# A planner's figures, a weight ring of six-block pieces and an ordered memory sum in a fused attention and MLP kernel

## Chip, cores, metric

One core of a Trainium2 chip. The metric is the device time of one execution in microseconds, median of several. Before: 692.45 us (3 runs, 692.03 to 692.54). The granted TensorE clock was 1.0.

## The reference, cut

A layer norm of `x` (2048 x 1024, bf16), then two branches whose results are added to `x`:

```python
xn = _layernorm(x)
# branch A: 32 heads of 32, four segments of 512 tokens with a running memory
q, k, v = xn @ wq, xn @ wk, xn @ wv
for s in range(4):
    p = softmax(qs @ ks.T * scale + causal mask); a_dot = p @ vs
    a_mem = (phi(qs) @ M) / (phi(qs) @ z + 1e-6)
    o = g * a_mem + (1 - g) * a_dot
    M += phi(ks).T @ vs ; z += sum(phi(ks))
# branch B: an MLP over the token axis, 2048 -> 3584 -> 2048
u = gelu(layernorm(xn).T @ w1 + b1); y = (u @ w2 + b2).T
return x + o @ wo + y
```

## The kernel before

A program on the host fixes the order of all instructions of all engines before anything runs. It keeps a clock for each engine (`fw.now`), books a duration for each instruction and each transfer, and at every point lets TensorE do what is ready by these books. I call this program the planner and its durations the books. From 214 us on, TensorE has two kinds of work: the attention chain (projections, bursts of logits, weighings), which waits for ScalarE, VectorE and POOL, and the fill: the matmuls of 32 output sums, whose w2 part by then needs only its weights, and whose wo part also an attention result. A gap in the chain is filled with fill matmuls.

Some words used below: a **row block** is 128 rows of w2, the weights of one fill matmul; a **piece** is what one transfer loads, four or six row blocks; a **ring** is the set of buffers that pieces pass through. A **burst** is the run of short matmuls that makes one step's logits, a **weighing** multiplies the exponentials with v, the **ost copy** evacuates its bank to SBUF, the **memory sum** adds that bank's `phi(k).T@v` to M and z. Cut to what the change touches:

```python
def dma(...):                                    # books of one transfer
    start = max(self.now[issuer], self.ready(reads, writes))
    self.now[issuer] = start + 450               # the issue
    self.q_free = max(start + 1900, self.q_free) + nbytes / 320 + (700 if transpose else 0)
    self.settle(self.q_free + 100 + ..., reads, writes)     # the landing
# ...
self.w2r = [e.take(f"w2n{i}", [P, 4, P], BF16) for i in range(6)]   # ring N of w2 pieces
self.w2l = [e.take(f"w2l{i}", [P, 6, P], BF16) for i in range(3)]   # ring L, sums worked on in single steps
# _Ring.ensure(b): when piece b is first asked for, load up to piece b + depth
# weigh(u, qb): a bank gets p@v, phi(q)@M and, in the last quarter of a segment, phi(k).T@v
fl.op({"dve": (tensor_copy ps->ost, 150 + n * 35, ...),   # whichever engine is free first by the books
       "act": (activation Copy ps->ost, 230 + n * 27, 200 + n * 27)}, [], [self.R_ost[o][qb]], box=box, give=not upd)
if upd:                                                   # memory sum, from the same bank
    fl.op({"dve": (MZ32 += ps, 283, 320)}, [self.R_MZ32[g]], [self.R_MZ32[g]], box=box, give=True)
```

`give=True` is where the books return the bank. A rule beneath all this makes readers of one bank on different engines wait for each other with semaphores; the planner's books did not contain that rule.

The softmax here doesn't subtract the row's maximum and nothing guards it: scores larger than these inputs give would overflow.

Of the kernel before, what the change touches and what calls it, by code (L numbers as in the profile page):

```python
# [18 lines left out]
P = 128  # L19
# [84 lines left out]
class FW:  # L104
# [121 lines left out]
    def dma(self, out_ap, in_ap, reads=(), writes=(), is_output=False, issuer="sp", extra=(),  # L226
            record_reads=True, transpose=False):
        es = self.E[issuer]
        nbytes = 2
        for x in out_ap.shape:  # L230
            nbytes *= x
        start = max(self.now[issuer], self.ready(reads, writes))
        self.now[issuer] = start + 450
        self.q_free = max(start + 1900, self.q_free) + nbytes / 320 + (700 if transpose else 0)
        self.settle(self.q_free + 100 + (600 if transpose else 0), reads, writes)
        self.log[issuer].append((start, self.q_free - start, writes[0].name if writes else ""))
        if not is_output:
            i = self.dma_next
            while self.dma_counts[i] and not self.slot_waiters[i]:
                i = (i + 1) % self.N_DMA_SEMS  # L240
            self.dma_next = (i + 1) % self.N_DMA_SEMS
            extra = list(extra) + self.slot_waiters[i]
            self.slot_waiters[i] = []
        self._waits(es, reads, writes, extra)
        assert not (es.pending_slots and issuer != "sp"), f"issuer {issuer} waited pool dma sem"
        es.pending_slots = []
        ins = es.eng.dma_start(out_ap, in_ap, transpose=True) if transpose else es.eng.dma_start(out_ap, in_ap)  # L247
        if is_output:
            j = self.out_next
            assert j < self.N_OUT_SEMS, "too many output dmas"  # L250
            self.out_next += 1
            ins.then_inc(self.out_sems[j], 16)
            tok = _Tok(("outdma", j), self.out_sems[j], 16)
            self.out_toks.append(tok)
        else:
            self.dma_counts[i] += 16
            ins.then_inc(self.dma_sems[i], 16)
            tok = _Tok(("dma", i), self.dma_sems[i], self.dma_counts[i])
        self._record(tok, reads if record_reads else (), writes)
        return tok  # L260
# [105 lines left out]
class _Flow:  # L366
# [1 line left out]

    LOOK = 5
    MARGIN = 120  # L370
    MARGIN_STEP = 80
    PART = 200

    def __init__(self, fw, R_bank, free, fill):
        self.fw, self.R_bank, self.free, self.fill = fw, R_bank, free, fill
# [208 lines left out]
class _Kernel:  # L584
# [95 lines left out]
    def over_early(self):  # L680
        fw = self.fw
        e = _Arena(self.nc, self.early_base, self.early_end)
        wait = _after(*self.R_xin, *self.R_xnt)
        self.wv_sb = e.take("wv_sb", [P, N_DCH, D_MODEL], BF16)
        self.wqr = [e.take(f"wq{i}", [P, N_DCH, P], BF16) for i in range(2)]
        self.wkr = [e.take(f"wk{i}", [P, N_DCH, P], BF16) for i in range(2)]
        self.w2r = [e.take(f"w2n{i}", [P, 4, P], BF16) for i in range(6)]
        self.w2l = [e.take(f"w2l{i}", [P, 6, P], BF16) for i in range(3)]
        self.w2s = [e.take(f"w2s{i}", [P, P], BF16) for i in range(2)]
        self.prod = e.take("prod", [P, 4, P], BF16)  # L690
        self.R_prod = Res("prod", wait)
        self.o_s = [e.take(f"o_s{i}", [P, 4, P], BF16) for i in range(2)]
        self.R_os = [Res(f"o_s{i}", wait) for i in range(2)]
        self.R_wv = [Res(f"wv{i}", wait) for i in range(2)]
        self.R_wq = [Res(f"wq{i}", wait) for i in range(2)]
        self.R_wk = [Res(f"wk{i}", wait) for i in range(2)]
        self.R_w2 = [Res(f"w2n{i}", wait) for i in range(6)]
        self.R_w2l = [Res(f"w2l{i}", wait) for i in range(3)]
        self.R_w2s = [Res(f"w2s{i}", wait) for i in range(2)]
        self.pkT = e.take("pkT", [P, SEG_L], BF16)  # L700
        self.etmp = e.take("etmp", [P, SEG_L], BF16)
        self.R_pkT = Res("pkT", wait)
        self.R_etmp = Res("etmp", wait)
        self.wq_ring = _Ring(fw, [t[:] for t in self.wqr], self.R_wq)
        self.wk_ring = _Ring(fw, [t[:] for t in self.wkr], self.R_wk)
        for i in range(N_UNIT):
            g = i % N_GRP
            self.wq_ring.srcs.append(self.A_wq[:, g * P:(g + 1) * P].rearrange("(dc p) j -> p dc j", p=P))
            self.wk_ring.srcs.append(self.A_wk[:, g * P:(g + 1) * P].rearrange("(dc p) j -> p dc j", p=P))
        self.fill = _Fill(self)  # L710
        self.wq_ring.ensure(0)
        self.wk_ring.ensure(0)
        for bv in range(2):
            fw.dma(self.wv_sb[:, :, bv * 512:(bv + 1) * 512],
                   self.A_wv[:, bv * 512:(bv + 1) * 512].rearrange("(dc p) j -> p dc j", p=P), writes=[self.R_wv[bv]])
# [311 lines left out]
        return self.flow.pe(mms, [R_w] + self.R_xnT[4 * s:4 * s + 4])[0]  # L1027

    def evac(self, dst, R_dst, box, view=lambda x: x):
        self.flow.op({"act": (lambda e, b: e.activation(dst, view(self.bank(b)), ACT.Copy), 635, 560),  # L1030
                      "dve": (lambda e, b: e.tensor_copy(dst, view(self.bank(b))), 690, 727)},
                     [], [R_dst], box=box, give=True, prio=0)

# [68 lines left out]
    def step(self, items):  # L1102
# [44 lines left out]
        pT, R = self.pT, self.R_pT  # L1147
        for i, (r, blocks, slot, masks) in enumerate(items):
            fl.op({"act": (lambda e, b, slot=slot: e.activation(pT[:, slot, :], self.bank(b), ACT.Exp, scale=SCALE),  # L1149
                           620, 530)}, [], [R[slot]], box=box[i], give=True)  # L1150
            v = pT[:, slot, :].rearrange("p (j q) -> p j q", q=P)
            if len(masks) > 1:
                ap, pat = v[:, masks[0]:masks[1] + 1:masks[1] - masks[0], :], [[0, 2], [1, P]]
            else:
                ap, pat = v[:, masks[0], :], [[1, P]]
            ns = 180 + 115 * len(masks)
            fl.op({"pool": (lambda e, ap=ap, pat=pat: e.affine_select(ap, ap, pattern=pat, compare_op=ALU.is_ge,  # L1157
                                                                      fill=0.0, base=0, channel_multiplier=-1),
                            ns, ns + 30)}, [R[slot]], [R[slot]])

    def weigh(self, u, qb):
# [19 lines left out]
        def mms(b):  # L1181
# [9 lines left out]
            if upd:  # L1191
# [5 lines left out]
        n = 8 if s else 4  # L1197
        dst = self.ost[o][:, 8 * qb:8 * qb + n, :].rearrange("p a x -> p (a x)")
        fl.op({"dve": (lambda e, b: e.tensor_copy(dst, self.ps[:, b, 0:n * VW]), 150 + n * 35, 185 + n * 35),  # L1199
               "act": (lambda e, b: e.activation(dst, self.ps[:, b, 0:n * VW], ACT.Copy), 230 + n * 27, 200 + n * 27)},  # L1200
              [], [self.R_ost[o][qb]], box=box, give=not upd, prio=0)
        if upd:
            m32, mbf = self.MZ32[:, g, :], self.MZbf[:, g, :]
            dg = self.diag[:].rearrange("p r x -> p (r x)")
            if s == 0:
                fl.op({"dve": (lambda e, b: e.tensor_copy(m32, self.ps[:, b, 2 * GW:3 * GW]), 283, 320)},
                      [], [self.R_MZ32[g]], box=box, give=True, prio=0)
            else:
                fl.op({"dve": (lambda e, b: e.tensor_tensor(m32, m32, self.ps[:, b, 2 * GW:3 * GW], op=ALU.add), 283, 320)},
                      [self.R_MZ32[g]], [self.R_MZ32[g]], box=box, give=True, prio=0)  # L1210
            fl.op({"dve": (lambda e: e.tensor_tensor(mbf, m32, dg, op=ALU.mult), 296, 330)},
                  [self.R_MZ32[g], self.R_diag], [self.R_MZbf[g]], prio=2)

    def combine(self, u):
# [17 lines left out]
        else:  # L1232
# [7 lines left out]
            for k, to, R_to in ((0, os, R_os), (1, self.prod, self.R_prod)):  # L1240
# [1 line left out]
                rk = rec.rearrange("p (q k r) -> p q k r", q=4, k=2)[:, :, k, :].unsqueeze(3)  # L1242
                pk = to[:].rearrange("p q (r d) -> p q r d", d=D_HEAD)
                dve(lambda e, v=v, rk=rk, pk=pk: e.tensor_tensor(pk, v, rk.to_broadcast([P, 4, 4, D_HEAD]), op=ALU.mult),
                    R_ost + [R_rec], [R_to], 640)
            dve(lambda e: e.tensor_tensor(os[:], os[:], self.prod[:], op=ALU.add), [R_os, self.R_prod], [R_os], 424)
        oT, R_oT = self.oT[s % 2], self.R_oT[s % 2][g]
        R_old = self.R_xnT[0:4] if s == 1 else []
# [9 lines left out]
    def attention_and_out(self):  # L1258
# [43 lines left out]
                else:  # L1302
                    break
        goals = [0, 0]
        knots = [(0, 0)] + [(last[8 * s + 7] + 2, 222 + 285 * s) for s in range(3)]
        knots += [(len(steps) - 1, self.fill.total - self.RESERVE), (len(steps), self.fill.total - 3)]
        for i in range(1, len(steps) + 1):
            (x0, y0), (x1, y1) = next((k0, k1) for k0, k1 in zip(knots, knots[1:]) if k0[0] <= i <= k1[0])
# [163 lines left out]
class _Fill:  # L1472
    KEEP = 5
    PLAIN = 12
    SOON = 600

    def __init__(self, k):
        self.k = k
        self.closed = []
        long = []  # L1480
        rest = [(c, half, False, 0) for c in range(12, 16) for half in range(2)]
        for j in range(3):
            g = [(c, half, True) for c in range(4 * j, 4 * j + 4) for half in range(2)]
            long += [x + (1,) for x in g[:3]]
            rest += [x + (0,) for x in g[3:]]
        long[-1] = long[-1][:3] + (0,)
        self.L = _Stream(k, self, long, "L", k.w2l, k.R_w2l, 2, [3])
        self.N = _Stream(k, self, rest, "N", k.w2r, k.R_w2, 4, [0, 1, 2])
        self.streams = [self.L, self.N]
        self.total = self.L.total() + self.N.total()  # L1490

# [107 lines left out]
```

## Time and profile before

| | before |
|---|---|
| time, us | 692.45 |
| span of the profile, us | 690.6 |
| PE / ACT / DVE / POOL busy, us | 685.7 / 299.7 / 241.2 / 152.8 |
| holes between 20 us and the tail, us | 1.23 (from the matmuls' starts) |

How to read it: a **hole** is what two neighbouring TensorE instructions start further apart than the same pair does undisturbed. The busy share hides holes under 163 ns; the prediction shows why, and shows the lines.

### The profile page before, as it was taken

The numbers are of one execution on the slowest core, as the hardware profiler recorded it, in microseconds if no ns is written. First come the engines' busy times: TensorE is split into PE (matmuls) and PEld (weight loads), VectorE is DVE, ScalarE is ACT, GpSimd is POOL, SyncE is SP. The second block draws the span as 40 slices with busy tenths as digits, with TensorE's granted clock in tenths as the row PEclk, the third lists the DMA queues.
The fourth block names the chain that finished last, engine by engine and source line by source line (L and its number), as shares of the span: only waits on it lengthen the run. The fifth ranks groups of instructions, "written<-read, shape, count | busy, mean of one in ns | idle before, by whom it ended". The sixth has DMA issues, their size and how long they took to land.

```text
span 690.6 us, 12093 instructions
## 1 busy us (share of the span) xinstructions
PE 685.7 (99%) x4846; PEld 328.2 (48%) x4846; DVE 241.2 (35%) x545; ACT 299.7 (43%) x571; POOL 152.8 (22%) x379
## 2 busy tenths in 40 slices
PE   8999999999999999999999999999999999999998
PEld 3444444444444544544455444544545544454544
DVE  6731100000002433443454462643534633351535
ACT  7331111111136456565365335644744644544540
POOL 5820000000001233223133113312321322313230
PEclk9999999999999999999999999999999999999999
DMA  9367666325037557656556556455554445637334
GB/s 316 112 178 183 158 159 204 94 61 138 1 100 168 137 126 175 142 136 157 119 131 150 118 129 150 97 138 136 140 130 116 119 104 136 148 86 130 92 78 141
DMA packets 275698, 92.04 MB, mean 133 GB/s; under 512 B 234171, under 2 KB 272059, under 8 KB 275643
## 3 DMA queue, kind: packets, MB, share of 16 engines
q1 hardware_dynamic: 275642, 91.28, 53.5%
q8 instruction: 38, 0.62, 0.4%
q14 instruction: 18, 0.14, 0.1%
HBM read 74.47 MB, written 5.24 MB: 115 GB/s over the span
## 4 chain that ended last, share of the span: by engine, by line
PE 97%; ACT 1%; DMA 1%; POOL 0%; DVE 0%; issue 0%; SPq 0%; POOLq 0%; DVEq 0%
PE ps_all L217 97%; DMA w2n<-in_B_w_dram 1%; ACT xn_tmp L849 0%; DMA xin<-in_A_x_dram 0%; ACT xn_tmp L851 0%; POOL pT L1157 0%; DVE h L890 0%; ACT pT L1149 0%; POOL ln_r L882 0%; SPq L247 0%; POOLq L580 0%; DVE fin L1342 0%; POOL ln_t L880 0%; DVE ln_mv L865 0%; DVEq L65 0%
## 5 line engine op out<-in xcount | busy, mean ns | idle before, releaser
L1157 POOL TENSOR_SCALAR_AFFINE_SELECT pT<-pT 128x256 bf16<-128x256 bf16 (+1 forms) x320 | 126.4, 403 | 507.7 <-ACT pT L1149 497.5
L1149 ACT ACTIVATE pT<-ps_all 128x512 bf16<-128x512 f32 x320 | 163.7, 614 | 76.8 <-PE ps_all L217 76.8
L217 PE MATMUL ps_all<-h,w1all 128*128 128x512 bf16 x896 | 193.9, 379 | 0.8 <-DVE h L890 0.7
L217 PE MATMUL ps_all<-gT,w2n 128*128 128x512 bf16 x644 | 151.3, 379 | 0.2 <-DMA w2n<-in_B_w_dram 0.2
L217 PEld LDWEIGHTS ps_all<-h,w1all 128*128 128x128 bf16 x896 | 87.5, 98 | 107.2 <-DMA w1all<-in_B_w_dram 1.0
L1004 ACT ACTIVATE gT<-ps_all,bc 128x512 bf16<-128x512 f32 x56 | 37.7, 690 | 140.7 <-PE ps_all L217 140.7
L217 PEld LDWEIGHTS ps_all<-gT,w2n 128*128 128x128 bf16 x644 | 59.6, 98 | 68.4 <-issue 3.1
L217 PE MATMUL ps_all<-gT,w2l 128*128 128x512 bf16 x244 | 63.7, 380 | 0.0
L217 PE MATMUL ps_all<-xnT,wq 128*128 128x512 bf16 x256 | 60.5, 379 | 0.0
L217 PE MATMUL ps_all<-xnT,wk 128*128 128x512 bf16 x256 | 60.5, 379 | 0.0
L217 PE MATMUL ps_all<-wv_sb,xnT 128*128 128x512 bf16 x256 | 60.1, 379 | 0.0
L1462 DVE SCALAR_TENSOR_TENSOR stg<-ps_all,bc,stg 128x512 bf16<-128x512 f32 x32 | 24.0, 750 | 99.2 <-PE ps_all L217 99.1
L217 PEld LDWEIGHTS ps_all<-vA,pT 128*128 128x128 bf16 x1280 | 45.3, 96 | 15.5 <-POOL pT L1157 0.6
L217 PE MATMUL ps_all<-vA,pT 128*128 128x33 bf16 x1280 | 46.3, 177 | 0.1
L1200 ACT ACTIVATE ost<-ps_all 128x264 bf16<-128x264 f32 (+1 forms) x56 | 19.8, 366 | 58.2 <-PE ps_all L217 57.1
L942 DVE TENSOR_SCALAR gcol<-gcol 128x32 f32<-128x32 f32 x1 | 0.2, 181 | 118.5 <-ACT gcol L940 118.5
L217 PEld LDWEIGHTS ps_all<-wv_sb,xnT 128*128 128x128 bf16 x256 | 25.0, 98 | 30.2
L217 PEld LDWEIGHTS ps_all<-xnT,wk 128*128 128x128 bf16 x256 | 25.0, 98 | 30.0
L1199 DVE CAST ost<-ps_all 128x264 bf16<-128x264 f32 (+1 forms) x72 | 28.0, 393 | 31.4 <-PE ps_all L217 31.1
L217 PEld LDWEIGHTS ps_all<-xnT,wq 128*128 128x128 bf16 x256 | 24.7, 98 | 29.3 <-issue 0.8
L1030 ACT ACTIVATE kT<-ps_all 128x512 bf16<-128x512 f32 x29 | 17.3, 597 | 46.2 <-PE ps_all L217 46.2
L217 PEld LDWEIGHTS ps_all<-gT,w2l 128*128 128x128 bf16 x244 | 21.2, 97 | 24.9 <-issue 6.0
(75 smaller groups left out, 492.8 us busy)
## 6 DMA issues: line engine op xcount, KB each, us to landing
w2n<-in_B_w_dram SPq DMA_DIRECT2D x161, 128.0 KB, 2.8
w1all<-in_B_w_dram SPq DMA_DIRECT2D x12, 1024.0 KB, 5.2
wq<-in_A_wq_dram SPq DMA_DIRECT2D x32, 256.0 KB, 2.8
wk<-in_A_wk_dram SPq DMA_DIRECT2D x32, 256.0 KB, 3.1
w2l<-in_B_w_dram SPq DMA_DIRECT2D x36, 192.0 KB, 2.9
stg<-in_A_x_dram SPq DMA_DIRECT2D x32, 128.0 KB, 2.9
out_dram<-stg SPq DMA_DIRECT2D x32, 128.0 KB, 1.8
xin<-in_A_x_dram SPq DMA_DIRECT2D x5, 512.0 KB, 6.7
```

What stands on the lines that cost most here:

```text
L217: ins = self.nc.tensor.matmul(out, *args, **kwargs)
L942: fw.op("dve", lambda e: e.tensor_scalar(self.gcol[:], self.gcol[:], 1.0, None, op0=ALU.add), reads=[self.R_gcol], writes=[self.R_gcol])
L1004: fw.op("act", lambda e: e.activation(self.gT[:, fc, half * 512:(half + 1) * 512], self.bank(b), ACT.Gelu_apprx_tanh, bias=self.b1c[:, fc: ...
L1030: self.flow.op({"act": (lambda e, b: e.activation(dst, view(self.bank(b)), ACT.Copy), 635, 560), "dve": (lambda e, b: e.tensor_copy(dst, v ...
L1149: fl.op({"act": (lambda e, b, slot=slot: e.activation(pT[:, slot, :], self.bank(b), ACT.Exp, scale=SCALE), 620, 530)}, [], [R[slot]], box= ...
L1157: fl.op({"pool": (lambda e, ap=ap, pat=pat: e.affine_select(ap, ap, pattern=pat, compare_op=ALU.is_ge, fill=0.0, base=0, channel_multiplie ...
L1199: fl.op({"dve": (lambda e, b: e.tensor_copy(dst, self.ps[:, b, 0:n * VW]), 150 + n * 35, 185 + n * 35), "act": (lambda e, b: e.activation( ...
L1200: "act": (lambda e, b: e.activation(dst, self.ps[:, b, 0:n * VW], ACT.Copy), 230 + n * 27, 200 + n * 27)},
L1462: engs={"dve": (lambda e, b: e.scalar_tensor_tensor(dst, k.bank(b), k.b2c[:, c:c + 1], dst, op0=ALU.add, op1=ALU.add), 750, 785)},
```

## The change

Its intent: bring the books nearer to what the trace shows, load w2 in fewer and larger pieces, make the books know that the memory sum follows the copy, and find the knobs anew for the order that results. The knobs: `MARGIN_STEP` is how long before now a burst's inputs must be booked ready, `PART` how much later its last bank may come free, `knots` how many fill matmuls are to be done by the end of each segment, and `SOON` how near the chain's next work must be for the planner to hold back ring N.

```diff
-        self.now[issuer] = start + 450
+        self.now[issuer] = start + (1200 if transpose else 620)
-    MARGIN_STEP = 80
-    PART = 200
+    MARGIN_STEP = 110
+    PART = 160
-        self.w2r = [e.take(f"w2n{i}", [P, 4, P], BF16) for i in range(6)]
+        self.w2r = [e.take(f"w2n{i}", [P, 6, P], BF16) for i in range(4)]
-        evac:  "act": ..., 635, 560
+        evac:  "act": ..., 600, 540
-        exponential: 620, 530
+        exponential: 620, 488
-        ost copy: "act": ..., 230 + n * 27, 200 + n * 27
+        ost copy: "act": ..., 175 + n * 27, 140 + n * 27
         if upd:
+            R_o = self.R_ost[o][qb]
-                      [self.R_MZ32[g]], [self.R_MZ32[g]], box=box, give=True, prio=0)
+                      [R_o, self.R_MZ32[g]], [self.R_MZ32[g]], box=box, give=True, prio=0)
-        products of combine: 640
+        products of combine: 700
-        knots = ... 222 + 285 * s
+        knots = ... 216 + 285 * s
-    SOON = 600
+    SOON = 700
-        self.N = _Stream(k, self, rest, "N", k.w2r, k.R_w2, 4, [0, 1, 2])
+        self.N = _Stream(k, self, rest, "N", k.w2r, k.R_w2, 3, [0, 1, 2])
```

(Cut: the same edit of the first segment's memory sum and of the ring's semaphores; two lines that change places without effect.)

More of the change, by code (lines that the diff above doesn't have):

```diff
@@ L696, in over_early @@
         self.R_wk = [Res(f"wk{i}", wait) for i in range(2)]
-        self.R_w2 = [Res(f"w2n{i}", wait) for i in range(6)]
+        self.R_w2 = [Res(f"w2n{i}", wait) for i in range(4)]
         self.R_w2l = [Res(f"w2l{i}", wait) for i in range(3)]
@@ L1029, in evac @@
     def evac(self, dst, R_dst, box, view=lambda x: x):
-        self.flow.op({"act": (lambda e, b: e.activation(dst, view(self.bank(b)), ACT.Copy), 635, 560),
+        self.flow.op({"act": (lambda e, b: e.activation(dst, view(self.bank(b)), ACT.Copy), 600, 540),
                       "dve": (lambda e, b: e.tensor_copy(dst, view(self.bank(b))), 690, 727)},
@@ L1149, in step @@
             fl.op({"act": (lambda e, b, slot=slot: e.activation(pT[:, slot, :], self.bank(b), ACT.Exp, scale=SCALE),
-                           620, 530)}, [], [R[slot]], box=box[i], give=True)
+                           620, 488)}, [], [R[slot]], box=box[i], give=True)
             v = pT[:, slot, :].rearrange("p (j q) -> p j q", q=P)
@@ L1199, in weigh @@
         fl.op({"dve": (lambda e, b: e.tensor_copy(dst, self.ps[:, b, 0:n * VW]), 150 + n * 35, 185 + n * 35),
-               "act": (lambda e, b: e.activation(dst, self.ps[:, b, 0:n * VW], ACT.Copy), 230 + n * 27, 200 + n * 27)},
+               "act": (lambda e, b: e.activation(dst, self.ps[:, b, 0:n * VW], ACT.Copy), 175 + n * 27, 140 + n * 27)},
               [], [self.R_ost[o][qb]], box=box, give=not upd, prio=0)
         if upd:
+            R_o = self.R_ost[o][qb]
             m32, mbf = self.MZ32[:, g, :], self.MZbf[:, g, :]
@@ L1206, in weigh @@
                 fl.op({"dve": (lambda e, b: e.tensor_copy(m32, self.ps[:, b, 2 * GW:3 * GW]), 283, 320)},
-                      [], [self.R_MZ32[g]], box=box, give=True, prio=0)
+                      [R_o], [self.R_MZ32[g]], box=box, give=True, prio=0)
             else:
                 fl.op({"dve": (lambda e, b: e.tensor_tensor(m32, m32, self.ps[:, b, 2 * GW:3 * GW], op=ALU.add), 283, 320)},
-                      [self.R_MZ32[g]], [self.R_MZ32[g]], box=box, give=True, prio=0)
+                      [R_o, self.R_MZ32[g]], [self.R_MZ32[g]], box=box, give=True, prio=0)
             fl.op({"dve": (lambda e: e.tensor_tensor(mbf, m32, dg, op=ALU.mult), 296, 330)},
@@ L1244, in combine @@
                 dve(lambda e, v=v, rk=rk, pk=pk: e.tensor_tensor(pk, v, rk.to_broadcast([P, 4, 4, D_HEAD]), op=ALU.mult),
-                    R_ost + [R_rec], [R_to], 640)
+                    R_ost + [R_rec], [R_to], 700)
             dve(lambda e: e.tensor_tensor(os[:], os[:], self.prod[:], op=ALU.add), [R_os, self.R_prod], [R_os], 424)
@@ L1304, in attention_and_out @@
         goals = [0, 0]
-        knots = [(0, 0)] + [(last[8 * s + 7] + 2, 222 + 285 * s) for s in range(3)]
+        knots = [(0, 0)] + [(last[8 * s + 7] + 2, 216 + 285 * s) for s in range(3)]
         knots += [(len(steps) - 1, self.fill.total - self.RESERVE), (len(steps), self.fill.total - 3)]
@@ L1479, in __init__ @@
         self.closed = []
+        rest = [(c, half, False, 0) for c in range(12, 16) for half in range(2)]
         long = []
-        rest = [(c, half, False, 0) for c in range(12, 16) for half in range(2)]
         for j in range(3):
```

## The prediction

> **What bounds the kernel now.** I read the page's busy shares first, then the stretches of time, then the waits, and last the single matmuls' start times in the trace, because TensorE's busy share alone cannot say how full it is. From the page and its costliest groups:
>
> ```profile
> PE 685.7 (99%) x4846; PEld 328.2 (48%) x4846; DVE 241.2 (35%) x545; ACT 299.7 (43%) x571; POOL 152.8 (22%) x379
> L217 PE MATMUL ps_all<-gT,w2n 128*128 128x512 bf16 x644 | 151.3, 379 | 0.2 <-DMA w2n<-in_B_w_dram 0.2
> ```
>
> TensorE is busy 99%, nothing else is over 43%. But one 512-column matmul is shown as 379 ns long, while in the trace two such matmuls start 216 ns apart when nothing holds them (mean 215.99 ns over 2694 pairs). A hole of up to 379 - 216 = 163 ns is therefore invisible in the busy share. So I took the distances between starts. The stretches (us, then busy time of PE, PEld, DVE, ACT, POOL) show where whole holes lie:
>
> ```profile
> 0.00:20.00 20.00, 17.96 (x74) 7.37 (x75) 13.73 (x32) 16.24 (x29) 10.81 (x31) 1.00 0.93 325
> 600.00:660.00 60.00, 59.79 (x495) 29.11 (x494) 23.19 (x48) 27.53 (x56) 15.93 (x39) 1.00 0.54 116
> 660.00:680.00 20.00, 19.89 (x164) 9.83 (x163) 8.67 (x19) 4.56 (x10) 3.84 (x9) 1.00 0.37 106
> 680.00:691.00 11.00, 8.15 (x46) 4.20 (x44) 5.22 (x9) 0.00 (x0) 0.00 (x0) 0.99 0.28 96
> ```
>
> Of the 4.9 us in which PE is not busy (690.6 - 685.7), 2.0 lie in the start and 2.4 after the last matmul, where the last result is added and stored. The change touches neither.
>
> By starts, the span adds up like this: 1.3 us until the first matmul; 652.8 us if every full-array matmul took n/2.4 + 2.6 ns (at least 25.3), which the undisturbed pairs do; 25.3 us in the 46 bursts of logits (45 of them take 542 to 549 ns, one 722); 4.4 us to enter them (46 x 96 ns); 4.2 us of holes; 2.6 us of tail. Of the 4.2, 3.0 are warm-up and first rows before 12.2 us. What is left for any new order to win is five holes and the long burst: 62 ns at 428.6 us, 204 at 444.6, 377 at 602.4, 143 at 627.7, 268 at 671.5, and 722 - 545 = 177 at 368.4. **Sum: 1.23 us, 0.18% of the time.** That is the central number here.
>
> Who causes them? The weight loads' waits name some:
>
> ```profile
> PEld ps_all L217 <- DMA w2n<-in_B_w_dram: 2.1, 5, 0.7
> PEld ps_all L217 <- ACT ost L1200: 1.5, 4, 0.4
> PEld ps_all L217 <- POOL pT L1157: 0.6, 1, 0.6
> ```
>
> Three of the holes (62 + 377 + 143 = 582 ns) lie between two matmuls on w2n pieces: the next piece had not landed. The largest, in the order of time on the DMA-issuing queue and, below, on TensorE:
>
> ```profile
> 596.35 1.20 SPq L247 DMA_TRANSPOSE xnT<-o_s  x1
> 597.59 0.58 SPq L247 DMA_DIRECT2D wq<-in_A_wq_dram  x1
> 598.22 0.58 SPq L247 DMA_DIRECT2D stg<-in_A_x_dram  x1
> 598.84 0.43 SPq L247 DMA_DIRECT2D wk<-in_A_wk_dram  x1
> 599.32 3.87 SPq L247 DMA_DIRECT2D w2n<-in_B_w_dram  x6
> ```
> ```profile
> 603.00 0.98 PEld L217 LDWEIGHTS ps_all<-gT,w2n 128*128 128x128 bf16 x6 [0.70 <-DMA w2n<-in_B_w_dram]
> ```
>
> The queue spends 599.32 - 596.35 = 2.97 us on four other issues before it gets to w2n. The kernel's own planner, which fixes the order of all instructions at build time, books 450 ns for each: 1.8 us. So it believed the piece to be there 1.2 us too soon and lined up a run of w2n matmuls that had to stop. The long burst:
>
> ```profile
> 367.83 0.39 ACT L1200 ACTIVATE ost<-ps_all 128x264 bf16<-128x264 f32 x1 [8.36 <-PE ps_all L217]
> 368.33 0.29 DVE L1209 TENSOR_TENSOR MZ<-MZ,ps_all 128x132 f32<-128x132 f32 x1 [0.43 <-PE ps_all L217]
> 368.74 0.09 PEld L217 LDWEIGHTS ps_all<-gT,w2s 32*128 32x128 bf16 x1 [0.26 <-issue]
> ```
>
> ACT reads the weighing's bank until 368.22, only then VectorE adds the memory sum from the same bank (until 368.62), and the burst's second half starts 0.12 us after that. The planner had no such order in its books and thought the bank free earlier. 582 + 177 = 759 ns of the 1.23 us are thus misjudgements of the two kinds that the change corrects. The hole at 671.5 is a mask on POOL; that at 444.6 ends 0.1 us after an exponential gives back a bank (my reading; the profile names no releaser).
>
> **What the Trainium skill says.** "TensorE: Matmul & The Clock Gate", Back-to-back issue gap, gives N/2.4 + 2.5 ns, 216 ns for 512 columns: this trace agrees (215.99), so the matmuls are at their own pace. "Perfetto Trace Analysis", Identifying the Most-Contended Engine, warns that matmul busy time is a poor measure of distance to the roofline; here it hides gaps under 163 ns. "PSUM — Partial Sum Buffer", PSUM bank collisions, says that two engines must be kept apart on one bank, ScalarE reads against VectorE reads included; that is why the kernel makes the memory sum wait, and in the trace it starts 101 ns after the end of ACT's evacuation in all three cases where ACT did it. "DMA: Bandwidth & Descriptors", Anatomy of one DMA, has a fixed part near 2 us and a part that grows with the bytes (for the GpSimd path); the trace's landings from SyncE fit the shape:
>
> ```profile
> w2n<-in_B_w_dram SPq DMA_DIRECT2D x161, 128.0 KB, 2.8
> w2l<-in_B_w_dram SPq DMA_DIRECT2D x36, 192.0 KB, 2.9
> ```
>
> **The change part by part.**
>
> *Pieces of six row blocks, four buffers, three ahead.* The same 24 row blocks of buffer and the same bytes in rows of the same length. A sum of 28 row blocks needs 5 pieces (6, 6, 6, 6, 4) in place of 7: 23 sums x 5 = 115 issues for 161, 46 fewer, at the median 505 ns of an issue in the trace 23 us of queue time, spread over 450 us. That queue isn't the bound. What counts is lead. Before, the load of piece b+4 stands in the program where b begins, 4 x 4 = 16 row blocks ahead of its use: 16 x 216 = 3.46 us in an unbroken run. After, it is 3 x 6 = 18: 3.89 us. It needs 2.8 us before and, judged by the 192 KB pieces of the other stream, 2.9 after: slack from 0.66 to 0.99 us. Against it: the new load goes to the buffer that was read just before (b-1), where the old one had a buffer to spare (b-2), so it can never be issued early when the queue happens to be idle. An unbroken sum lasts 28 x 216 = 6.05 us, and its issues take 2.5 us of it in place of 3.5, so a backlog like the one above clears sooner.
>
> *The books.* An issue 620 ns in place of 450, a transpose 1200: for the run above 1200 + 3 x 620 = 3.06 us against 2.97 measured. Evacuations 600 (measured 597 to 603), exponentials 488 apart (477 measured), ost copies 175 + 27n, thus 391 and 283 (measured 389 and 281), the o_s products 700 (698 and 737). Every one moves towards the trace. I expect most of the 582 ns to go: 450.
>
> *The memory sum behind the weighing's evacuation.* In the trace before all 24 memory sums already come after it, so no order turns over. New is a wait: where VectorE does both (21 of 24) the sum starts 81 to 85 ns before the copy's end, and will start some 34 ns after it, as dependent VectorE instructions here do: 21 x 117 ns = 2.5 us of an engine that is 35% busy, and a bank back 0.12 us later, 21 times, beside other work. For the three on ACT nothing changes but that the planner knows. Gain: the 177 ns.
>
> *The new spread (216 for 222, 110 for 80, 160 for 200, 700 for 600).* These move matmuls in time and remove none: six fewer fill matmuls before each of the first three knots and six more at the end. Matmuls, bursts, slices and their entry costs stay. It deals the order anew, and with it new chances for small misses. The old order had six holes of 205 ns in the mean; I allow for one new hole, 0.1 to 0.2 us, and count none of the 204 + 268 = 472 ns that no part addresses as won.
>
> Sum: 0.45 + 0.18 of the addressed 0.76 won, 0.1 to 0.2 lost: 0.5 us. 692.45 - 0.5 = **691.9 us**.
>
> **The rivals.** (1) *A new wait in place of the old*: the tighter buffer, or other transfers held up in the one issuing queue behind a w2n load that waits for TensorE. For it: that queue waited 326 us for PE already. Against: the read it waits for directly precedes the place where it is issued. If each of some ten extra bank or load waits costs 0.1 to 0.2 us, the time is 693 to 694. (2) *The fill runs dry*: six matmuls moved to the end could leave an earlier stage short (6 x 216 = 1.3 us at most per knot); against it, the trace before has no hole of that size. Then 693.5. (3) *Everything hidden anyway*: the misses go but others of the same size appear; then 692.4, and runs cannot tell it from before, whose three times spread over 0.5 us. (4) *A real win*: would need to shorten matmuls, start or tail; nothing here does. All six holes gone makes 691.2.
>
> **Range and chances.** The low end is the floor, 692.45 - 1.23, less 0.2 of spread between runs: 691.0. The high end is rival 1 or 2 in full: 693.4. Two per cent are 13.8 us, eleven times what all holes hold, and on the slow side some 67 new holes of the mean size: faster 0.005, slower 0.01.
>
> **What would show it.** Right: 115 w2n issues of at most 192 KB; no hole over 300 ns at a w2n matmul; no burst over 600 ns beside a memory sum; sum of starts' excess between 20 us and the last matmul under 1.2 us; start and tail unchanged within 0.1 us. Wrong: more than ten holes, or a wait for w2n of over 0.5 us, or stretches between 200 and 680 us with PE under 99.5% busy.

## The result

691.79 us (6 runs, 691.43 to 692.30) against 692.36 (6 runs of before, the three above among them): ratio 0.9993, interval 0.9980 to 1.0005, the same within 2%. A ratio is the mean time of one kernel's fast runs over that of the other's of the same rounds, so not quite the ratio of the medians quoted.

Part 1 of the page of the changed kernel, busy time of each engine:

```profile
PE 680.5 (99%) x4765; PEld 328.6 (48%) x4846; DVE 226.8 (33%) x500; ACT 313.5 (45%) x616; POOL 153.2 (22%) x379
```

Two things are to be seen. TensorE has 4765 matmul records for 4846 weight loads: 81 records are missing, about one in sixty, so its 680.5 us is no gain and a 216 ns gap in the matmuls means nothing here. From here on **I measure holes at the starts of the weight loads**, which are complete; these come out up to 10 ns larger than in the prediction (71, 205, 385, 153, 278 and 176 ns in place of 62, 204, 377, 143, 268 and 177). And 14 us of work went from VectorE to ScalarE. The groups that did it, before and then after:

```profile
L1200 ACT ACTIVATE ost<-ps_all 128x264 bf16<-128x264 f32 x44 | 16.5, 389 | 54.4 <-PE ps_all L217 53.8
L1200 ACT ACTIVATE ost<-ps_all 128x132 bf16<-128x132 f32 x12 | 3.4, 281 | 3.8 <-PE ps_all L217 3.3
```
```profile
L1200 ACT ACTIVATE ost<-ps_all 128x264 bf16<-128x264 f32 x70 | 26.6, 405 | 71.3 <-PE ps_all L217 70.8
L1200 ACT ACTIVATE ost<-ps_all 128x132 bf16<-128x132 f32 x29 | 8.4, 302 | 10.5 <-PE ps_all L217 10.3
```

ScalarE does 99 of the 128 ost copies in place of 56: booked cheaper, it is chosen more often. Hence ScalarE reads the bank before the memory sum in 23 of 24 cases, in place of 3. The prediction did not see this. What it had asked of the profile: 115 w2n issues (92 of 192 KB and 23 of 128), as said; no burst over 600 ns, as said; no w2n hole over 300 ns, which failed. One of its signs of being wrong appeared too: a wait for w2n of over 0.5 us (0.87 in the weight load's line below; the kernel before had one of 0.70). Its sign by TensorE's busy share can't be read here, as records are missing.

The holes after: the long burst and the 204 ns hole are gone, but the largest hole of all is at a w2n piece. The DMA-issuing queue before it, and the weight load that waited:

```profile
576.10 0.37 SPq L247 DMA_DIRECT2D stg<-in_A_x_dram  x1
576.99 2.30 SPq L247 DMA_TRANSPOSE xnT<-o_s  x1
579.33 1.17 SPq L247 DMA_DIRECT2D w2n<-in_B_w_dram  x2
```
```profile
582.12 0.98 PEld L217 LDWEIGHTS ps_all<-gT,w2n 128*128 128x128 bf16 x6 [0.87 <-DMA w2n<-in_B_w_dram]
```

The transpose took 2.30 us to issue, where 1200 ns are booked and 1.2 us is usual; the w2n issues behind it came 0.8 us later than planned and TensorE stood 554 ns. The other hole is the last weighing's, behind the masks on POOL:

```profile
669.46 2.33 POOL L1157 TENSOR_SCALAR_AFFINE_SELECT pT<-pT 128x256 bf16<-128x256 bf16 x4
669.84 0.88 DVE L1245 TENSOR_TENSOR prod<-ost,srec 128x512 bf16<-128x512 bf16 x1
671.47 0.17 PEld L217 LDWEIGHTS ps_all<-vA,pT 128*128 128x128 bf16 x4 [0.81 <-POOL pT L1157]
```

The masks that began while VectorE multiplied from two SBUF operands took 726 and 852 ns. The first, which began before the product, took 406 and the last, beside no product, 401 (booked 410). The products took 832 and 884 (booked 700). "SBUF — State Buffer", Who interferes with whom, says that a VectorE instruction with two SBUF inputs contends with a GpSimd instruction that reads SBUF; this agrees.

But the masks took as long in the kernel before (408, 729 and 852 ns), where this hole was 278 ns and not 491. What differs is the fill between the last burst and the hole: nine w2l matmuls in both, then four wo matmuls before and three after. One matmul less is the 213 ns. The last weight loads ahead of the hole, before and then after:

```profile
670.68 0.74 PEld L217 LDWEIGHTS ps_all<-wo_sb,oT 128*128 128x128 bf16 x4
```
```profile
670.13 0.53 PEld L217 LDWEIGHTS ps_all<-wo_sb,oT 128*128 128x128 bf16 x3
```

### The profile page after: what moved, and what is told of

It is laid out like the page before. It is cut to its first block, busy times and chain, and to the rows that moved or that the text cites. A ratio compares the mean times of both kernels' runs of the same rounds, so it can differ in the third digit from the quotient of the medians.

```text
span 690.2 us, 11956 instructions
## 1 busy us (share of the span) xinstructions
PE 680.5 (99%) x4765; PEld 328.6 (48%) x4846; DVE 226.8 (33%) x500; ACT 313.5 (45%) x616; POOL 153.2 (22%) x379
## 4 chain that ended last, share of the span: by engine, by line
PE 96%; issue 1%; ACT 1%; DMA 1%; POOL 0%; DVE 0%; SPq 0%; POOLq 0%; DVEq 0%
PE ps_all L217 96%; DMA xin<-in_A_x_dram 0%; DMA w2n<-in_B_w_dram 0%; ACT xn_tmp L851 0%; ACT xn_tmp L849 0%; POOL pT L1157 0%; DVE h L890 0%; POOL ln_r L882 0%; ACT pT L1149 0%; SPq L247 0%; DVE qT L1031 0%; POOLq L580 0%; DVE fin L1343 0%; POOL ln_t L880 0%; POOL ln_t L877 0%
## 5 line engine op out<-in xcount | busy, mean ns | idle before, releaser
L217 PE MATMUL ps_all<-gT,w2n 128*128 128x512 bf16 x618 | 146.8, 379 | 2.2 <-issue 0.5
L1200 ACT ACTIVATE ost<-ps_all 128x264 bf16<-128x264 f32 (+1 forms) x99 | 35.0, 375 | 81.8 <-PE ps_all L217 81.0
L217 PE MATMUL ps_all<-xnT,wq 128*128 128x512 bf16 x248 | 58.9, 379 | 0.4
L217 PE MATMUL ps_all<-gT,w2l 128*128 128x512 bf16 x226 | 57.8, 380 | 1.1 <-issue 0.5
L1030 ACT ACTIVATE kT<-ps_all 128x512 bf16<-128x512 f32 x32 | 19.1, 597 | 60.6 <-PE ps_all L217 60.5
L1015 DVE TENSOR_SCALAR etmp<-etmp 128x512 bf16<-128x512 bf16 x48 | 14.1, 293 | 55.1 <-ACT etmp L1014 55.1
```

Of the source, the lines that this page charges most:

```text
L217: ins = self.nc.tensor.matmul(out, *args, **kwargs)
L1015: fl.op({"dve": (lambda e: e.tensor_scalar(et[:], et[:], 1.0, None, op0=ALU.min), 294, 330)}, [R_et], [R_et], prio=2)
L1030: self.flow.op({"act": (lambda e, b: e.activation(dst, view(self.bank(b)), ACT.Copy), 600, 540), "dve": (lambda e, b: e.tensor_copy(dst, v ...
L1200: "act": (lambda e, b: e.activation(dst, self.ps[:, b, 0:n * VW], ACT.Copy), 175 + n * 27, 140 + n * 27)},
```

## The experiments

Twelve runs. The theory after the result: the time is the sum of a few holes, each a place where the books are wrong or where the planner itself idles; the parts of the change act on different ones. Rivals: a new order has holes of the usual size somewhere else; a hole is the run's, not the kernel's. By building the kernels one can read what the planner books as its own idling of TensorE: 0.18 us near 444.5 us before, none after. In the table, "long bursts" is what bursts took beyond the usual 545 ns, "planned idling" the holes where the planner books idling, "w2 pieces" those where a piece had not landed, "last masks" the one before the last weighing. Times of a single run (state unknown) are weak evidence beside a spread of 0.5 us between runs of one kernel; the verdicts rest on the holes. Summary, in ns:

| kernel | time, us | long bursts | planned idling | w2 pieces | last masks | all holes |
|---|---|---|---|---|---|---|
| before, 1st profile | 692.45 | 176 | 205 | 609 | 278 | 1269 |
| before, again | 692.24 | 175 | 204 | 711 | 275 | 1366 |
| after, 1st | 691.79 | 0 | 0 | 625 | 491 | 1116 |
| after, again | 691.60 | 0 | 0 | 272 | 498 | 770 |
| after, timed | 691.91 | 0 | 0 | 650 | 491 | 1141 |
| before + issue books | 692.00 | 176 | 204 | 312 | 282 | 974 |
| before + order | 692.31 | 0 | 607 | 522 | 276 | 1406 |
| before + ring | 691.41 | 174 | 204 | 0 | 282 | 660 |
| before + ring, timed | 691.74 | 174 | 204 | 0 | 275 | 653 |
| before + engine books | 695.12 | 1940 | 0 | 1229 | 498 | 3668 |
| after, old ring | 692.27 | 0 | 0 | 703 | 492 | 1196 |
| after, no order | 694.95 | 1823 | 0 | 1371 | 495 | 3690 |
| late w2n, slow masks | 691.94 | 0 | 0 | 883 | 0 | 883 |
| both rings late, slow masks | 691.20 | 0 | 205 | 0 | 0 | 205 |

**The kernel before, again.** No edit.

> The kernel before, unchanged, for a second profile: how much of what one profile shows is the kernel's and how much the run's. Theory A (most holes come from the fixed order): the long burst at 368.4 us (+177 ns) and the hole at 444.6 us (204 ns) come back within 40 ns, and the three holes at w2n pieces (62, 377, 143 ns) come back too, 450 to 700 ns in sum. Rival B (the w2n holes are the run's, from issues that happen to take long): burst and the hole at 444.6 come back, but the w2n holes sum to something else by over 200 ns or lie elsewhere. Time 692.0 to 692.6 either way.

Burst and the 204 ns hole returned to within 1 ns. The w2n holes summed to 711 ns: those near 602 (334) and 627 us (126) again, that at 428 not, and a new one of 251 at 580. Neither theory holds alone: place and rough size are the order's, the rest is the run's.

**The changed kernel, again.** No edit.

> The changed kernel, unchanged, for a second profile. Its first had holes of 62, 544 (both at w2n pieces) and 482 ns (the last weighing, waiting for masks on POOL). Theory A: all three come back, 950 to 1200 ns in sum. Rival B: the hole of 544 ns, before which one transpose took 2.3 us to issue where others take 1.2, is gone or is under 150 ns; the one of 482 ns at the masks comes back, since no transfer is in it. Time 691.4 to 692.3 either way.

Rival B held: 107 ns in place of 554 at 581.2 us. The same transpose had taken 1.83 us. A hole of 165 appeared at 531.9, behind a transpose of 2.2 us. The one at the masks came back (498).

**Issue books alone.**

```diff
 # on before
-        self.now[issuer] = start + 450
+        self.now[issuer] = start + (1200 if transpose else 620)
```

> The kernel before with only the planner's figures for an issue changed (620 ns, and 1200 for a transpose, in place of 450). My prediction's step: the planner now knows that the w2n pieces come later, so the holes at w2n pieces fall from 582 ns to under 150. The rival, from the changed kernel's own profile (606 ns of such holes in spite of the new figures): they stay at 300 to 700 ns, as the delays that cause them are longer than the new figures. The long burst (+177) and the 204 ns hole should stay in both, for nothing here touches them. Time: 691.9 by the first, 692.4 by the second.

312 ns left, all near 602 us: some half of the 609 and 711, so not nearly all went and my step was too large. The rival's band held. These holes vary by up to 380 ns between profiles of one kernel (272 and 650 in the table), and the new figures also deal the order anew, so one profile cannot say how much of the fall is theirs.

**The order alone.**

```diff
 # on before
-                      [self.R_MZ32[g]], [self.R_MZ32[g]], box=box, ...
+                      [R_o, self.R_MZ32[g]], [self.R_MZ32[g]], box=box, ...
```

> The kernel before with only the memory sum ordered behind its weighing's evacuation. My prediction's step: the long burst of 722 ns is gone (all 46 bursts at most 560 ns), the rest as before, so 0.18 us is won. The rival: the planner, which now returns those banks later in its own reckoning, runs out of work that it may place; it books 0.7 us of idling near 399, 445, 525 and 527 us in place of 0.18 us at 444.5, so holes appear there, of 100 to 500 ns in sum beyond those of before, and the time is 692.5 to 693.0.

The burst is gone, as I had predicted. But the rival is right on what it costs: 205 at 398.3, 204 at 444.3, 145 and 53 near 525 us, all where the planner books idling. 607 - 204 = 403 ns lost for 176 won; only the time, 692.31, fell short of its band.

**The ring alone.**

```diff
 # on before
-  [P, 4, P] x 6 buffers, depth 4
+  [P, 6, P] x 4 buffers, depth 3
```

> The kernel before with only the ring changed: four buffers of six row blocks, three ahead, in place of six of four, four ahead. The planner's idling is the same as before (0.18 us near 444.5), so burst and that hole should come back. My prediction's step: more lead (18 row blocks for 16) and fewer issues, so the holes at w2n pieces, 609 and 711 ns in the two profiles of before, fall under 300. The rival: the pieces are late because the loads of q, k and x share the transfer engines at their limit just then, which the ring doesn't change, so the hole near 602 us stays at 300 to 400 ns.

No hole at any w2n piece; the other three are untouched. TensorE's list of work is the same as before's in every place, so nothing was dealt anew: this is the ring's effect alone.

**Engine books alone.**

```diff
 # on before: evac 600/540, exponential 620/488, ost copy on ACT 175 + n*27, products 700
```

> The kernel before with only the planner's figures for ScalarE and VectorE changed (evacuations 600/540, exponentials 488 apart, ost copies 175 + 27n, products 700). The theory that the 204 ns hole at 444.6 us is an idling which the planner itself put there, because by its old figures no bank was free: it books no idling at all with the new ones, so the hole goes, 0.2 us. The rival (my prediction counted none of it as won, a re-dealt order makes a hole of the like elsewhere): holes other than at w2n pieces stay at 600 to 700 ns in sum. The hole at the last masks near 671 us stays in both.

The 204 ns hole went, as said. I had not expected the rest: 2.8 us slower. Ten bursts are 174 to 177 ns longer than usual (one of them before's own) and three by about 65. The timeline of one:

```profile
502.29 0.39 ACT L1200 ACTIVATE ost<-ps_all 128x264 bf16<-128x264 f32 x1 [0.30 <-PE ps_all L217]
502.78 0.29 DVE L1209 TENSOR_TENSOR MZ<-MZ,ps_all 128x132 f32<-128x132 f32 x1 [1.11 <-PE ps_all L217]
503.19 0.09 PEld L217 LDWEIGHTS ps_all<-gT,w2s 32*128 32x128 bf16 x1 [0.25 <-issue]
```

It is the picture of before's burst at 368 us, tenfold: ScalarE copies until 502.68, VectorE's memory sum ends at 503.07, the burst's second half begins 0.12 us later. By the planner's list ScalarE now does 98 of the ost copies, and the books hold the bank to be free before it is. In all ten the burst begins 45 to 47 ns after its memory sum begins. In the changed kernel no burst begins sooner than 547 ns after its sum begins, and the sum is over by then:

```profile
432.77 0.39 ACT L1200 ACTIVATE ost<-ps_all 128x264 bf16<-128x264 f32 x1 [0.30 <-PE ps_all L217]
433.19 0.29 DVE L1210 TENSOR_TENSOR MZ<-MZ,ps_all 128x132 f32<-128x132 f32 x1 [0.72 <-ACT ost L1200]
433.74 0.27 PEld L217 LDWEIGHTS ps_all<-qT,kT 32*128 32x128 bf16 x9 [0.42 <-issue]
433.92 0.09 PEld L217 LDWEIGHTS ps_all<-gT,w2s 32*128 32x128 bf16 x1
```

Of the 2.35 us of holes that this kernel has more than before, 1.76 are in bursts, 0.57 at w2n pieces and 0.22 at the last masks, less the 0.2 of idling won. Four figures were changed at once; that the one for the ost copy sends the copies to ScalarE is read from the kernel, not tested.

**The changed kernel with the old ring.**

```diff
 # on after
-  [P, 6, P] x 4 buffers, depth 3
+  [P, 4, P] x 6 buffers, depth 4
```

> The changed kernel with the old ring (six buffers of four row blocks, four ahead). If the ring is what took the holes at w2n pieces from 609 and 711 ns to 625 and 272, they come back to 500 to 800. If the ring is idle and the issue figures did it (312 ns were left with them alone), they stay at 150 to 450. The planner books 10 ns of idling more, so nothing else should change; the hole of 480 to 500 ns at the last masks stays.

703 ns at w2n pieces, at three places. That is in the band for the ring, but little above the changed kernel's 625 and 650. So one profile does not show what the ring is worth in the changed order.

**Later landings, slower masks.**

```diff
 # on after
-  landing: q_free + 100
+  landing: q_free + 100 + 600 for tiles named w2n
+  in the last logit step, masks: 700
-    RESERVE = 60
+    RESERVE = 72
```

> The changed kernel with two more corrections of the planner's figures: w2n and the other w2 pieces are taken to land 600 ns later, and the masks of the last logit step take 700 ns in place of 410 or 295 (they took up to 852 in the changed kernel's profile), with 72 fill matmuls kept for the end in place of 60. If the remaining holes are misjudgements of just these two durations, the one at the last masks falls from 490 to under 150 ns and those at w2n pieces from 625 and 272 to under 150, all holes from 1116 and 770 to under 300, and the time is 690.9 to 691.3, ratio to before 0.9980 to 0.9988. If the order is merely dealt anew and misses of the usual size come up elsewhere, holes stay at 700 to 1100 and the ratio at 0.999 to 1.000.

Ratio 0.9999 (0.9985 to 1.0012), 691.94 us. The hole at the masks is gone, a w2n hole of 321 was left, and one of 562 came at a piece of the other ring, w2l. My edit had reached only w2n, although the text says all w2 pieces. An unbroken run on the L ring has 12 row blocks of lead, 12 x 216 = 2.6 us, less than the 2.9 us to landing. By the stated criterion the rival won this one.

**The changed kernel without the order.**

```diff
 # on after
-                      [R_o, self.R_MZ32[g]], ...
+                      [self.R_MZ32[g]], ...
```

> The changed kernel without its ordering of the memory sum, all the rest kept. In the kernel before with only the new engine figures, 9 bursts became 174 to 177 ns longer and 3 by 65, as ScalarE took 98 of the 128 ost copies in place of 56 and the planner did not know that the memory sum waits for them. If the order is what spares the changed kernel this, 7 or more bursts come out over 700 ns, 1.2 to 2 us in sum, beside 0.3 us of idling that the planner books near 525 us, and the time is 693.0 to 694.0. If the other figures (ring, issue, spread) spare it, at most 2 bursts are long and the time stays under 692.4.

Nine bursts of 173 to 177 ns and four of about 64, 1.82 us in sum; with 1.37 us at w2n pieces, 694.95 us, above the band. So it is the order that spares the changed kernel what its engine books would do. The idling booked near 525 us did not show, and the w2n holes grew more than foreseen (one of 935 ns, beside a transpose of 1.8 us); why, I did not settle.

**The ring alone, timed.** The edit of the ring alone.

> The kernel before with only the ring changed, once more and timed; its one profile had no hole at a w2n piece, where before had 609 and 711 ns. If that is the ring's, this profile has under 150 ns of them too, holes in all 600 to 800 ns, and the time is 691.4 to 691.9, ratio 0.9985 to 0.9995. If that was a lucky run, they come back to 300 to 700 and the ratio is 0.9995 to 1.0005. The burst (+175), the 204 ns hole and the one at the last masks (280) recur in both.

Again none at w2n pieces, 653 ns in all; 691.74 us, ratio 0.9988 (0.9974 to 1.0002), so the time alone does not tell it from before. None in two profiles of two was hardly luck. The queue and the load on the transfers at the place near 600 us, first the kernel before (its second profile), then the ring alone:

```profile
599.34 3.87 SPq L247 DMA_DIRECT2D w2n<-in_B_w_dram  x6
```
```profile
600.00:604.00 4.00, 3.84 (x19) 1.58 (x17) 0.00 (x0) 0.00 (x0) 0.00 (x0) 1.00 1.10 259
```
```profile
599.83 4.25 SPq L247 DMA_DIRECT2D w2n<-in_B_w_dram  x4
```
```profile
600.00:604.00 4.00, 4.00 (x21) 1.79 (x19) 0.00 (x0) 0.00 (x0) 0.00 (x0) 1.00 0.91 219
```

In both the queue was busy with other loads until 599.3. Before had 5 pieces x 4 = 20 row blocks on hand when the unbroken run began at 598.1, then issued six pieces end to end with the transfer engines full (share 1.10). The ring has no spare buffer, so all 4 x 6 = 24 were on hand, and its next piece, issued at 599.83, was not needed before 603.3: the issues stand 1.295 us apart, each waiting for TensorE to free a buffer, and nothing waits for them. Over the whole run the shortest time from a piece's issue to its first use was 2.40 us before and 3.48 with the ring.

**The changed kernel, timed.** No edit.

> The changed kernel, a third profile, timed on the same chip as the ring alone. Hole at the last masks 480 to 500 ns again; holes at w2n pieces anywhere from 100 to 650 ns as in its first two; no long burst. Ratio 0.9988 to 0.9998. If the whole gain of the change is the ring's, it is not faster than the ring alone by more than 0.2 us.

691.91 us, ratio 0.9989 (0.9977 to 1.0002); 597 and 53 ns at w2n pieces, 491 at the masks, no long burst. It is not faster than the ring alone. The 597 ns stand at 413.2 us, where the first profile had 71; the transpose ahead of it (409.0 us) took 2.45 us to issue there and 1.92 in the first.

**Both rings late, slow masks.**

```diff
 # on after
-  landing: q_free + 100
+  landing: q_free + 100 + 1200 for all w2 tiles
+  in the last logit step, masks: 700
-    RESERVE = 60
+    RESERVE = 84
```

> As the run with late landings before it, in which the edit reached only the w2n pieces though its text said all w2 pieces, and a hole of 562 ns appeared at a w2l piece at 668.7 us: now the pieces of both rings are taken to land 1200 ns later, the last step's masks take 700 ns, and 84 fill matmuls are kept for the end. The planner books 0.19 us of idling of its own. If late pieces and slow masks are all that is left, holes are 200 to 400 ns in sum, none at a w2 piece over 100, time 691.0 to 691.4, ratio 0.998 to 0.9987. If avoiding those waits only moves them, holes stay over 600 ns and the ratio at 0.999 to 1.000.

One hole is left, the planner's own idling of 205 ns at 398.3 us. The forecast held. The long transposes are still there (2.05 us at 409.2, 1.99 at 621.9), but TensorE has other work by then: at 409 us the changed kernel ran 28 w2n matmuls in a row and stopped after 18 of them, this one runs 24 without a stop and then eight of the k projection. The stretch that cost most before:

```profile
600.00:660.00 60.00, 60.00 (x498) 29.59 (x496) 22.30 (x45) 30.03 (x61) 17.77 (x42) 1.00 0.52 123
```

The busy share shows no gap there, and the weight loads show none either. 691.20 us, five runs from 691.11 to 691.36, all below every run of the changed kernel on that chip (691.56 to 692.09); ratio to before 0.9980 (0.9967 to 0.9992), a difference clear of the noise. It beats both kernels, the changed one by 0.7 us, with 0.94 us less of holes (205 in place of 1141 ns). Landings, masks and reserve were changed together; the holes at the pieces and at the masks vanish where each should act, but the three were not timed apart.

## Why the prediction was right, and where its steps were not

**The number and the bound held.** 691.79 against 691.9. What carried it was the sum of all that could be won, 1.23 us, from the starts of matmuls. The last experiment, which removes nearly all of it, gains about what that sum allows: 692.62 - 691.20 = 1.42 us by the medians of its rounds, where before's runs spread over 1.5 us. The profiles agree with the size: holes 1318 ns in the mean of two before, 1009 in the mean of three after, 0.31 us less; the spans, 690.55 and 690.15 in the mean, differ by 0.40, of which 0.1 us is the start (first w2n load at 214.16 and 214.06 us).

**That the number fits so well is partly luck.** The interval of the ratio reaches from 1.4 us less to 0.3 us more, so the time could not tell 0.5 us won from nothing. The holes say 0.31 us, made up otherwise than forecast: about 0.14 won at the w2n pieces (forecast 0.45), 0.18 at the long burst (0.18), 0.20 from the planner's idling (0), and 0.21 lost at the last masks (0.1 to 0.2 lost somewhere).

**The step "the books win 450 of the 582 ns at w2n pieces" failed.** In the changed kernel these holes are 625, 272 and 650 ns, 516 in the mean, against 660 before: about 0.14 us won. The issue books alone left 312 in their one profile, the ring alone none in two. In the changed order other runs of w2n follow transposes whose issue takes 1.8 to 2.4 us, which no booked figure foresaw.

**The ring: right sign, and a count that fits one order only.** I set a lead of 18 against 16 row blocks. What mattered near 600 us in the old order was the stock, 24 against 20 row blocks, and that issues no longer crowd. There the spare buffer which I held to be an advantage of the old ring was stock not loaded. In the changed order the lead of 18 is what counts: five of the six holes at w2n pieces in its three profiles come after exactly 18 row blocks in a row. The fourth piece stood in the queue behind the transpose and was issued 1.4 to 2.0 us after the run began, too late for the 18 x 216 = 3.89 us that three pieces last. By holes the ring alone (653 and 660 ns) does better than the whole change (1009).

**The memory sum: the 177 ns were won, the rest of the step was wrong.** I counted VectorE as the copier in 21 of 24 cases and a wait of 117 ns there. It copied in one. (With the order alone it copied in 22, and in 20 of these the sum came 34 to 35 ns after the copy, as forecast.) The step "every figure moves towards the trace", with no cost set against it, failed: truer engine figures gave ScalarE 42 more ost copies, and alone these figures cost 2.8 us, 1.76 of it in long bursts, because one rule was still missing in the books. The ordering is that rule; without it the changed kernel takes 694.95 us. Alone it loses 0.4 us in idling for 0.18 won. The two parts belong together.

The order does one thing more, which the prediction does not have: the memory sum starts sooner after ScalarE's copy, 32 to 33 ns in place of 100 to 103. Some 69 ns are too little for the 174 to 177 by which a burst was too long, and what moved is the burst itself: it begins 547 ns and more after the sum does, in place of some 46.

**The 472 ns of which I counted none as won.** Right in sum by two errors: the planner's idling (204) went, and the hole at the masks grew from some 278 to 491, by one fill matmul. The engine books alone bring that too (498); issue books, order and ring, each alone, leave 275 to 282.

**Rival 3** (misses of the same size appear elsewhere) described a part of what happened: near 580 and 413 us it is so. No rival's time was reached.

**What stays open.** Why the same few transposes take 1.5 to 2.9 us to issue in some runs and 1.2 in others. The knobs alone were not run, and which knob settles which idling I did not take apart; building showed only that the engine books alone book none, and that with the new knobs on the old books the planner would idle 1.5 us.

## What to carry to other kernels

When the bound engine is busy 99%, sum its holes start by start before arguing about a change: that sum bounds what a new order can win, and each hole says whose wait it is. In a kernel ordered by a model, a truer figure can cost time if a rule is missing beside it, since the model then uses the engine more in just the place where it errs; change figures and rules together. Book a transfer that varies by its late landings, not its median: in the last experiment that cost no hole beyond the planner's own 205 ns, while each late piece had stopped the engine.

## What the Trainium skill lacked or had wrong

- "TensorE: Matmul & The Clock Gate", Back-to-back issue gap, gives about 131 ns for 512 columns as the sustained rate of loads and matmuls in a real kernel, and 216 as an isolated gap. Sustained here: 215.99 ns over 2694 pairs. The isolated figure is the sustained one.
- "DMA: Bandwidth & Descriptors", DMA Transpose (X-bar), has no time for issuing one, and the page's counts of sequencer cycles, in a passage on trn3 B0, no spread. Here, after 200 us, SyncE is busy 1.2 us with one of 128 x 512 bf16 most times, and 1.5 to 2.9 us with a few, often the same ones from run to run (at 409 us: 1.92, 1.52, 2.45 and 2.05 us).
- "SBUF — State Buffer", Who interferes with whom, has two factors for a contention of the two engines (VectorE 6.8 times and GpSimd 1.5 times slower) without the instructions they belong to. Here masks that began beside a two-input product took 726 and 852 ns in place of 401 to 406, and the products 832 and 884 in place of 698.
- No page has a time for how soon VectorE's sum follows ScalarE's copy from one PSUM bank by semaphore: it started 101 to 102 ns after the copy's end in the kernel before and 32 to 33 ns after it in the changed one. The trace shows the difference: before, a separate semaphore instruction of 21 ns waits for ScalarE ahead of the sum, which itself waits for TensorE; after, the sum carries the one wait, for ScalarE, and no such instruction stands before it.
